# Attention with mixed heads and a folded expert layer on Trainium2: how the first block's score rows reach the softmax

## The chip, the cores and the metric

The kernel runs on one core of a Trainium2 chip. The metric is the device time of one execution in microseconds (us); three executions of the kernel before gave 1636.96, 1638.15 and 1639.79 us, a median of 1638.15 us. A core has TensorE (PE in the rows; PEld is its weight load), VectorE (DVE), ScalarE (ACT), GpSimd (POOL) and SyncE (SP, which in this kernel issues every transfer), and 16 DMA engines that all queues share.

## The reference

```python
scores = scale * np.matmul(q, k.transpose(0, 1, 3, 2))          # batch 8, heads 12, seq 448, dim 64
scores = np.einsum('bhij,hg->bgij', scores, w_pre)              # heads are mixed ahead of the softmax
scores = scores - np.max(scores, axis=-1, keepdims=True)
attn = np.exp(scores)
attn = attn / (np.sum(attn, axis=-1, keepdims=True) + 1e-09)
attn = np.einsum('bhij,hg->bgij', attn, w_post)                 # and mixed again behind it
x = np.matmul(attn, v) -> (3584, 768)
out = (((x @ w1) * (x @ w2)) @ w3) @ w_out                      # 768 -> 1024 -> 1024 -> 768
```

Inputs and result of the attention are float32; the expert weights arrive as 64-bit floats and are converted on the chip.

## The kernel before, in words

**The work is cut into steps.** One step handles 10 query rows of one batch with all 12 heads, so 120 rows of 448 scores; a batch has 45 steps (the code calls `t` a block of 10 rows, and the steps run on over 8 batches to N = 360). To mix heads, the 120 rows must lie on 120 partitions in the order (row, head). The scores are made per head with the query rows on the partitions, so they are written to a buffer in HBM, `raw_d[b]`, of the layout (row, head, column), and read back: `fetch(n)` (L209 to L218) loads the 10 x 12 rows of step n into the rows' tile `r`. In step n the main loop (L890 to L987) issues `fetch(n + 4)`, does `softmax(n)` (a row minimum on VectorE, L246, and an exponential on ScalarE, L249), `scale(n - 1)` (L258 to L262 on VectorE), `post(n - 2)` (four matmuls, L272, and a copy to `mt`, L278) and, last on TensorE, `mix(n + 1)` (L235 in the first 20 steps). All engines work their own instructions strictly in the order of the program.

**Batch 0 starts differently.** Its queries and keys come in six tiles `kq0s`, one for each pair of heads: a first part with the keys and the first 112 query rows (L773), and the other query columns later (`others(p)`, L866 and L867). `qk_first(p, c, banks)` (L149 to L168) makes the scores of pair p and of the c-th 112 query rows: two matmuls (L158), two copies from PSUM (L163 on ScalarE, L164 on VectorE for c = 0), and it hands back the store to `raw_d` (issued at L168). For c = 0 the copies go to one large tile, the score tile `sz` (112 rows x 12 heads x 448). Of it only the first 48 rows (FIRST) are stored by the six stores of L168; the store of the other 64 rows, one transfer of 1344 KB, is the line L800 (`held`). The stores for c = 0 trail the scores by two pairs (L792). The scores with c = 1 to 3 are made inside the main loop: the list `firsts` (L801 to L803) says which in which step. The first one of a step comes ahead of the other matmuls of the step, the others ahead of `mix`.

**Beside it runs the conversion of the weights**, `converting` (L124 to L145), one job in each step: a load of raw words on SP (`cs`, L96, three buffers, two jobs ahead), a square on ScalarE (L102) that waits for that load, four operations on VectorE (L112 to L116) and a step later a cast on ScalarE (L121) and a subtraction on GpSimd (L122). A job has two halves: the load, the cast and the subtraction of the job before, and the square are the first; VectorE's four operations are the second. In a step the first half stands ahead of `softmax(n)` (L944 against L947), the second behind `scale` (L961).

**Order on SP before the main loop**: six first parts of `kq0s`, the two mixing matrices (`wpre`, `wpo`), words of jobs 0 and 1; stores of pairs 0 to 3; words of job 2; stores of pairs 4 and 5; `others(0)`, `others(1)`; `fetch(0)`, `fetch(1)`, `fetch(2)`; words of job 3 (the first marked `wo`); the 1344 KB store; words of job 4; `fetch(3)`; `others(2)`. Step 0 begins with `fetch(4)`, which reads rows 40 to 49 and so waits for both kinds of stores.

Of the kernel before, what the change touches and what calls it, by code (L numbers as in the profile page):

```python
# [6 lines left out]
F32 = mybir.dt.float32  # L7
# [8 lines left out]
B, H, S, D = 8, 12, 448, 64  # L16
DM, FF = 768, 1024
HP = H // 2
IB = 10
GI = H * IB  # L20
NB = -(-S // IB)
JT, NJ = 112, 4
# [23 lines left out]
class Kernel:  # L46
# [102 lines left out]
    def qk_first(self, p, c, banks):  # L149


        nc, t = self.nc, self.kq0s[p]
        cols = slice(c * JT, (c + 1) * JT)
        q = slice(S + cols.start, S + cols.stop) if c else slice(0, JT)
        ps = [self.bank(i, f"psz{p}_{c}_{s}")[:JT, :S] for s, i in enumerate(banks)]
        for s in range(2):
            rows = slice(s * D, (s + 1) * D)
            nc.tensor.matmul(ps[s], t[rows, q], t[rows, JT:JT + S], start=True, stop=True)  # L158
        if c == 0:
            st = self.sz[:, 2 * p:2 * p + 2]  # L160
        else:
            st = (self.qp if p % 2 else self.kp).tile([JT, 2, S], F32, tag="st", name=f"sz{p}_{c}", bufs=2)
        nc.scalar.copy(st[:, 0], ps[0])  # L163
        (nc.scalar.copy if c else nc.vector.tensor_copy)(st[:, 1], ps[1])  # L164
        dst = self.raw_d[0][cols, 2 * p:2 * p + 2, :]
        if c == 0:
            dst, st = dst[:FIRST], st[:FIRST]
        return lambda: nc.sync.dma_start(dst, st)  # L168

# [572 lines left out]
    def run(self):  # L742
        nc, tc = self.nc, self.tc
# [29 lines left out]
            nc.sync.dma_start(self.kq0s[p][:, :JT + S], self.kq0[p][:, :JT + S])  # L773
        self.sz = self.mp.tile([JT, NJ, H, GB * IB], F32, tag="mt", name="sz")
        self.sz = self.sz.rearrange("p j g i -> p (j g i)")[:, :H * S].rearrange("p (h j) -> p h j", h=H)
        w = self.kp.tile([128, S], F32R, tag="qh", name="wpre_s").bitcast(F32)[:GI, :GI]
        self.wsc = cp.tile([GI, GI], F32, name="wsc")
        nc.sync.dma_start(w, self.wpre)
# [8 lines left out]
        self.wph = cp.tile([GI, GI], F32R, name="wph")  # L787
        self.wpl = cp.tile([GI, GI], F32R, name="wpl")
        held = []
        for p in range(HP):  # L790
            held.append(self.qk_first(p, 0, ((0, 1), (2, 3), (6, 7))[p % 3]))
            if p > 1:  # L792
                held.pop(0)()
        nc.vector.tensor_copy(self.wph, self.wsc)
        nc.vector.tensor_tensor(self.wpl, self.wsc, self.wph.bitcast(F32), op=ALU.subtract)
# [4 lines left out]
        held = lambda: nc.sync.dma_start(self.raw_d[0][FIRST:JT], self.sz[FIRST:])  # L800
        firsts = {}  # L801
        for u in range(HP, HP * NJ):
            firsts.setdefault((u - HP) * 15 // (HP * NJ - HP), []).append((u % HP, u // HP))  # L803

# [1 line left out]
        for b in range(1, B):  # L808
            first, per, ahead = (12, 26 / 48, 2) if b == 1 else ((b - 1) * NB - 6, 45 / 48, 3)
            for u in range(H * NJ):  # L810
                h, c = divmod(u, NJ)
                n = first + int(u * per)
# [10 lines left out]
        N = B * NB  # L823
# [29 lines left out]
        def advance(count):  # L853
            nonlocal done
            for _ in range(min(count, total - done)):
                next(background)
                done += 1

        def there(p):

            f, r = divmod(p - 3 - 2 * KF, 3)
            return 2 * KF * 3 * (1 + f) + (0, 9, 18)[r] if f >= 0 else min(max(3 * (p - 3), 0), KF * 3)

        wanted, LF, turn = 0, 4, itertools.chain((6, 7, 0) * 9, itertools.cycle((6, 7)))
        self.v_list = [(b, a, g) for b in range(B) for a in range(NG) for g in range(HP)]
        def others(p):  # L866
            nc.sync.dma_start(self.kq0s[p][:, JT + S:], self.kq0[p][:, JT + S:])  # L867

        others(0)
        others(1)  # L870
        for n in range(LF - 1):
            self.fetch(n)
        next(fold_pieces)
        next(fold_pieces)
# [15 lines left out]
        for n in range(N + 6):  # L890
            self.step = n
            if n == GB + 1:
                self.close("qp")
                self.xp = [self.pool("xp0", 1)]
            if n == SWITCH:
                assert done == total
                next(background, None)
                self.do_ends()
                self.do_soon()
                self.do_later()  # L900
                assert not fold_pieces
                self.close("fp")
                self.wp = self.pool("wp", 5, side="right")
                self.up = self.pool("up", 1, side="right")
                self.xp.append(self.pool("xp1", 1, side="right"))
                background, total, done = self.experts(phases), (E_1 + E_2) * ONE + P_1 * (B - ONE) // 2, 0
            if n == LATE:
                assert done >= E_1
                self.close("xp0", "cx")
                self.xq, self.cb = self.pool("xq", 2), self.pool("cb", 1)  # L910
            if n == PAIR:

                assert done >= 2 * E_1 + E_2 and unit_pieces is None and not self.jobs and not self.ys
                self.do_ends()
                self.do_soon()
                self.do_later()
                self.pairs, self.w_ahead = True, 4
                self.close("xp1", "cb", "xq", "cs")
                self.xq = self.pool("xq", 2)
                self.up2 = self.pool("up2", 1, side="right")  # L920
                self.free += range(N_UP, NS)
                setup = self.pair_setup(phases)
            if PAIR <= n < PAIR + 7:
                next(setup, None)
            if LF <= n + LF < N:
                self.fetch(n + LF)
            self.do_later()
            if n + 3 < HP:
                others(n + 3)
            elif 2 * HP - 3 <= n < 2 * HP:  # L930
                self.load_v()
            for x in loads.get(n, []):
                self.load_kq(*x)
            for x in splits.get(n, []):
                self.split_kq(*x, nc.gpsimd, nc.gpsimd)

            p, pieces = self.n_made - 1 if fold_pieces else 2 * KF + 3 * KF, None
            if avs.get(n):
                pass
            elif fold_pieces:  # L940
                f = (self.n_made - 1 - 2 * KF) // 3
                if f < 2 or done >= 2 * KF * 3 * (f - 1):
                    pieces = fold_pieces
                    if next(pieces, self) is self:  # L944
                        fold_pieces = pieces = None
            if n < N:
                self.softmax(n)  # L947
            if 0 <= n - 1 < N:
                self.scale(n - 1)
            if n + 2 < N:  # L950
                self.split_r(n + 2)
            self.do_soon()
            for x in firsts.get(n, [])[:1]:
                self.later.append(self.qk_first(*x, (next(turn), next(turn))))
            for x in qks.get(n, []):
                store = self.qk(*x, nq % 2, nc.scalar.copy)
                nq += 1
                if store:
                    self.later.append(store)
            if pieces:  # L960
                next(pieces)  # L961
            elif unit_pieces and not fold_pieces and not avs.get(n):
                ahead = 1 if n < SWITCH else 2 * done // (3 * K1) + 4 + (done > 0)
                if n_pieces < ahead:
                    n_pieces += 1
                    if next(unit_pieces, self) is self:
                        unit_pieces = None
                    else:
                        next(unit_pieces)
            now = share.get(n, 0)  # L970
            if n < SWITCH:

                wanted += now
                now = max(min(there(p), KF * 3 + wanted) - done, 0)
            self.do_sums()

            advance(now // 2)
            if 0 <= n - 2 < N:
                self.post(n - 2)
            for x in firsts.get(n, [])[1:]:  # L980
                self.later.append(self.qk_first(*x, (next(turn), next(turn))))
            for x in avs.get(n, []):
                self.av(*x)
            advance(now - now // 2)
            if n + 1 < N:
                self.mix(n + 1)
            self.do_ends()  # L987
# [68 lines left out]
```

## Time and profile before

| | |
|---|---|
| median of three runs | 1638.15 us (1636.96 to 1639.79) |
| the profiled execution | 1639.43 us, span 1637.7 us, so 1.7 us lie around the span |
| mean granted clock of TensorE | 0.993 of full speed |
| TensorE busy | 1579.9 us, 96% of the span |
| GpSimd, VectorE, ScalarE busy | 1068.5, 1030.6, 997.3 us (65%, 63%, 61%) |
| DMA | 446.10 MB, mean 272 GB/s, all on one queue |

A row of a group gives the engine, the line, the operation and the tiles (out<-in), how often it came, and its busy time; in brackets stands the idle time of the engine before it and what ended it. "SPq" is SP's queue: its times are those of issuing a transfer, not of moving the data. PEclk 1.00 is 2.4 GHz, 0.50 is 1.2 GHz.

### The profile page before, as it was taken

The page shows a single profiled execution, that of the slowest core. Times are in us where ns is not written, and L with a number is a line of the kernel's source. Part 1 is how long each engine was busy: PE and PEld are TensorE (multiplying, and loading weights), DVE is VectorE, ACT ScalarE, POOL GpSimd, SP SyncE. Part 2 cuts the span into 40 slices and gives each one's busy share as a digit, 9 for nine tenths or more (in the row PEclk, how much of TensorE's full clock was granted, in tenths as well). Part 3 has the DMA queues.
Part 4 walks back from the last instruction along what each step waited for, and adds up shares of the span by engine and source line. Part 5 has one row for each costly group of instructions (what it writes and reads, how often), then busy time and mean ns, then how long its engine had stood idle before and what let it go on. Part 6 is the DMA issues. An engine that isn't in the chain of part 4 may idle for free. (4 is left out here: it accounts for less than half of the span.)

```text
span 1637.7 us, 31687 instructions
## 1 busy us (share of the span) xinstructions
PE 1579.9 (96%) x10528; PEld 1414.0 (86%) x10528; DVE 1030.6 (63%) x2302; ACT 997.3 (61%) x2413; POOL 1068.5 (65%) x902
## 2 busy tenths in 40 slices
PE   5999999999999999999999999999999999999999
PEld 2578997887898888889899898899999898999988
DVE  5967768778747767863465565745555557634573
ACT  4877657677666776776666666666765554542321
POOL 1346546667657788885576776876675666655774
PEclk7999999999999999999999999999999999999999
DMA  8988879898899999999978977889978756678875
GB/s 263 342 269 275 255 223 302 277 310 288 264 279 310 321 341 315 323 335 306 312 240 279 290 243 238 257 270 309 305 248 250 238 188 196 211 229 302 281 233 179
DMA packets 233906, 446.10 MB, mean 272 GB/s; under 512 B 21838, under 2 KB 159054, under 8 KB 233678
## 3 DMA queue, kind: packets, MB, share of 16 engines
q1 hardware_dynamic: 233742, 444.08, 84.6%
q8 instruction: 83, 1.36, 0.4%
q14 instruction: 81, 0.66, 0.1%
HBM read 309.90 MB, written 134.09 MB: 271 GB/s over the span
## 5 line engine op out<-in xcount | busy, mean ns | idle before, releaser
L227 POOL TENSOR_TENSOR rl<-r,rh 120x448 fp32r<-120x448 f32 (+1 forms) x340 | 425.0, 1250 | 321.9 <-DVE rh L226 108.0
L246 DVE TENSOR_REDUCE mn<-psm 120x1 f32<-120x448 f32 x360 | 223.8, 622 | 410.1 <-PE psm L240 395.1
L249 ACT ACTIVATE e<-psm,mn 120x448 f32<-120x448 f32 x360 | 228.5, 635 | 348.1 <-DVE sa L258 293.4
L272 PEld LDWEIGHTS pso<-w,e 120*112 120x112 f32 (+1 forms) x2880 | 345.5, 177 | 49.4 <-ACT mt L278 35.0
L272 PE MATMUL pso<-w,e 120*112 120x120 f32 (+1 forms) x2880 | 358.9, 267 | 20.6 <-ACT mt L278 20.2
L703 PE MATMUL e<-eh,wu 128*128 128x448 f32 x1008 | 304.4, 371 | 1.1 <-DVE c L657 1.1
L278 ACT COPY mt<-pso 112x480 f32<-112x480 f32 x360 | 206.9, 575 | 14.9 <-PE pso L272 9.9
L703 PEld LDWEIGHTS e<-eh,wu 128*128 128x128 f32 x1008 | 187.3, 188 | 16.1 <-DVE c L657 1.9
L226 DVE CAST rh<-r 120x448 fp32r<-120x448 f32 (+1 forms) x340 | 189.9, 559 | 4.1 <-DMA r<-raw_d 3.0
L703 PE MATMUL e<-el,wu 128*128 128x448 f32 x504 | 187.6, 372 | 2.4 <-POOL el L642 2.4
L198 ACT COPY st<-psq 112x448 f32<-112x448 f32 x336 | 173.3, 527 | 25.8 <-DMA raw_d<-st 25.7
L303 PE MATMUL psa<-mt,v 112*64 112x150 f32 (+1 forms) x2304 | 156.9, 292 | 1.9 <-DMA v<-v 1.9
L183 POOL TENSOR_TENSOR ql<-kq,qh 128x448 fp32r<-128x448 f32 x84 | 99.2, 1181 | 85.1 <-ACT qh L181 84.9
L303 PEld LDWEIGHTS psa<-mt,v 112*64 112x64 f32 x2304 | 143.6, 137 | 8.1 <-DMA v<-v 2.3
L657 DVE TENSOR_TENSOR c<-c,e 128x448 f32<-128x448 f32 x168 | 101.2, 615 | 70.4 <-PE e L703 65.8
L193 PE MATMUL psq<-kk,qh 128*112 128x448 f32 x336 | 125.7, 374 | 8.0 <-ACT st L198 7.8
L238 PE MATMUL psm<-rh,wph 120*120 120x448 f32 (+1 forms) x340 | 129.6, 381 | 0.0
L523 PE MATMUL eg<-xh,wu 128*128 128x448 f32 x384 | 127.3, 381 | 0.0
L240 PE MATMUL psm<-rl,wph 120*120 120x448 f32 (+1 forms) x340 | 124.1, 365 | 0.6 <-POOL rl L227 0.5
L239 PE MATMUL psm<-rh,wpl 120*120 120x448 f32 (+1 forms) x340 | 124.2, 365 | 0.0
L194 PE MATMUL psq<-kk,ql 128*112 128x448 f32 x336 | 122.8, 365 | 0.0
L642 POOL TENSOR_TENSOR el<-x,eh 128x448 fp32r<-128x448 f32 x90 | 105.7, 1195 | 9.3 <-DMA x<-x_d 5.3
(114 smaller groups left out, 2961.7 us busy)
## 6 DMA issues: line engine op xcount, KB each, us to landing
r<-raw_d SPq DMA_DIRECT2D x352, 210.0 KB, 4.1
raw_d<-st SPq DMA_DIRECT2D x168, 392.0 KB, 4.7
wu<-w_d SPq DMA_DIRECT2D x104, 384.0 KB, 5.6
wu<-s_d SPq DMA_DIRECT2D x96, 384.0 KB, 4.4
v<-v SPq DMA_DIRECT2D x144, 224.0 KB, 5.1
kq<-kq SPq DMA_DIRECT2D x42, 672.0 KB, 7.0
wu<-w_d SPq DMA_DIRECT2D x51, 512.0 KB, 5.9
wu<-s_d SPq DMA_DIRECT2D x36, 512.0 KB, 4.4
```

The source lines that it names most:

```text
L193: nc.tensor.matmul(p, qh[:, cols], kk, start=True, stop=False)
L198: copy(st[:, c % 2], p)
L226: nc.vector.tensor_copy(rh[:K], r[:K])
L227: nc.gpsimd.tensor_tensor(rl[:K], r[:K], rh[:K].bitcast(F32), op=ALU.subtract)
L238: nc.tensor.matmul(p[:K, :S], self.wph[:K, :K], rh[:K], start=True, stop=False)
L246: nc.vector.tensor_reduce(mn[:K], p[:K, :S], axis=AX.X, op=ALU.min)
L249: nc.scalar.activation(e[:K], p[:K, :S], AF.Exp, bias=mn[:K], scale=-1.0, accum_out=sm[:K])
L272: nc.tensor.matmul(p[:, j, :, :w], e[:K, j * JT:(j + 1) * JT], w2[:K, :, :w], start=True, stop=True)
L278: self.ends.append((4, lambda: copy(dst, p[:, :, :, :w])))
L303: nc.tensor.matmul(self.psa[rows, g % 3, :W], v[:, j, rows], mt[:, j, 2 * g + s, :W], start=(j == 0), stop=(j == NJ - 1))
L523: nc.tensor.matmul(p, u[:, k % (K1 // 2), x], xs[y][:, k], start=(k == 0 and t == 0), stop=(k == K1 - 1 and t == 2))
L703: nc.tensor.matmul(p, w[:, k, x], ops[m, k][y], start=(k == 0 and t == 0), stop=(k == nk - 1 and t == 2))
```

## The change

Four edits.

- The rows of step 0 no longer go through HBM. After the scores of pair p are copied for c = 0, each of its two heads sends its first 10 rows of the score tile to partitions h, h + 12, ... of the rows' tile `rs[0]`. That makes twelve transfers of 10 x 1792 bytes, the even heads issued by GpSimd, the odd ones by SP. `fetch(0)` is left out. `raw_d` is still written in full.
- The stores of the first 48 rows trail the scores by three pairs, not two; and `others(0)` is issued ahead of `wpre`, not behind the stores.
- In `firsts` the second set of scores with c = 1 (pair 1) moves from step 0 to step 1; all later ones stay in their steps.
- In steps 0 to 3 `softmax(n)` stands ahead of the first half of the conversion job.

```diff
@@ qk_first
         dst = self.raw_d[0][cols, 2 * p:2 * p + 2, :]
         if c == 0:
+
+            for h in range(2 * p, 2 * p + 2):
+                (nc.sync if h % 2 else nc.gpsimd).dma_start(self.rs[0][h::H], self.sz[:IB, h])
             dst, st = dst[:FIRST], st[:FIRST]
         return lambda: nc.sync.dma_start(dst, st)
@@ run
         self.sz = self.sz.rearrange("p j g i -> p (j g i)")[:, :H * S].rearrange("p (h j) -> p h j", h=H)
+        nc.sync.dma_start(self.kq0s[0][:, JT + S:], self.kq0[0][:, JT + S:])
         w = self.kp.tile([128, S], F32R, tag="qh", name="wpre_s").bitcast(F32)[:GI, :GI]
...
         held = []
+        self.rs[0] = self.rp.tile([GI, S], F32, tag="r", name="r0", bufs=3)
         for p in range(HP):
             held.append(self.qk_first(p, 0, ((0, 1), (2, 3), (6, 7))[p % 3]))
-            if p > 1:
+            if p > 2:
                 held.pop(0)()
...
         for u in range(HP, HP * NJ):
-            firsts.setdefault((u - HP) * 15 // (HP * NJ - HP), []).append((u % HP, u // HP))
+            firsts.setdefault((u - HP - 1) * 14 // (HP * NJ - HP - 1) + 1, []).append((u % HP, u // HP))
...
-        others(0)
         others(1)
-        for n in range(LF - 1):
+        for n in range(1, LF - 1):
             self.fetch(n)
...
                 self.split_kq(*x, nc.gpsimd, nc.gpsimd)
+            if n < 4:
+                self.softmax(n)
...
-            if n < N:
+            if 4 <= n < N:
                 self.softmax(n)
```

## Rows read from the trace of the kernel before

**Rows 1.** The page: busy share (PE) and DMA share in 40 equal slices.

```profile
PE   5999999999999999999999999999999999999999
DMA  8988879898899999999978977889978756678875
```

**Rows 2.** Windows: us, busy PE, PEld, DVE, ACT, POOL, PEclk, DMA share, GB/s.

```profile
0.00:10.00 10.00, 6.26 (x17) 2.91 (x19) 1.75 (x4) 2.88 (x4) 0.20 (x4) 1.00 0.81 264
10.00:16.70 6.70, 1.96 (x11) 0.71 (x7) 5.68 (x13) 3.00 (x6) 0.67 (x1) 1.00 0.85 202
18.30:24.10 5.80, 3.92 (x8) 1.42 (x8) 1.92 (x5) 0.83 (x3) 1.72 (x2) 0.55 1.01 290
29.30:33.50 4.20, 1.61 (x4) 0.48 (x4) 2.52 (x5) 1.16 (x3) 0.00 (x0) 0.50 0.75 165
31.80:37.20 5.40, 5.31 (x10) 1.41 (x10) 2.44 (x7) 2.46 (x6) 1.00 (x1) 0.50 0.97 286
33.50:64.00 30.50, 30.32 (x143) 16.74 (x142) 25.64 (x58) 23.33 (x55) 7.02 (x7) 0.94 0.99 341
130.00:1600.00 1470.00, 1440.30 (x9832) 1317.86 (x9833) 927.36 (x2074) 909.33 (x2213) 1011.02 (x845) 1.00 0.86 273
```

**Rows 3.** Timeline of TensorE, 17 to 45 us.

```profile
20.18 1.82 PE L235 MATMUL psm<-r,wsc 120*120 120x448 f32 x2 [8.21 <-DMA r<-raw_d]
21.93 2.54 PE L158 MATMUL psz<-kqz 64*112 64x448 f32 x6
...
26.71 1.64 PE L235 MATMUL psm<-r,wsc 120*120 120x448 f32 x2
31.89 1.84 PE L158 MATMUL psz<-kqz 64*112 64x448 f32 x4 [3.54 <-DMA kqz<-kq]
```

**Rows 4.** Timeline of SP's queue, 0 to 30 us: issues.

```profile
9.08 2.67 SPq L168 DMA_DIRECT2D raw_d<-sz  x4
...
12.84 1.36 SPq L168 DMA_DIRECT2D raw_d<-sz  x2
...
17.39 1.25 SPq L217 DMA_DIRECT2D r<-raw_d  x3
...
19.15 0.61 SPq L800 DMA_DIRECT2D raw_d<-sz  x1
...
20.43 2.21 SPq L217 DMA_DIRECT2D r<-raw_d  x1
22.68 2.52 SPq L867 DMA_DIRECT2D kqz<-kq  x1
```

**Rows 5.** DMA issues near 13, 19 and 22.7 us: KB each, us to landing.

```profile
raw_d<-sz SPq DMA_DIRECT2D x2, 168.0 KB, 3.7
...
raw_d<-sz SPq DMA_DIRECT2D x1, 1344.0 KB, 10.1
...
kqz<-kq SPq DMA_DIRECT2D x1, 168.0 KB, 9.1
```

**Rows 6.** Timeline of VectorE, 8 to 36 us.

```profile
8.24 0.22 DVE L786 TENSOR_SCALAR wsc<-wpre_s 120x120 f32<-120x120 f32 x1 [8.24 <-DMA wpre_s<-wpre]
...
10.50 2.13 DVE L164 COPY sz<-psz 112x448 f32<-112x448 f32 x3 [0.44 <-PE psz L158]
...
19.37 0.42 DVE L116 SCALAR_TENSOR_TENSOR cx<-cm,ca 128x256 f32<-128x256 f32 x1
...
24.16 0.56 DVE L112 TENSOR_SCALAR ca<-cs 128x384 int32<-128x384 int32 x1 [1.50 <-DMA cs<-wo]
```

**Rows 7.** Waits in the first 45 us: total, times, longest.

```profile
ACT cm L102 <- DMA cs<-wo: 8.4, 4, 3.9
```

**Rows 8.** Timeline of ScalarE, 19 to 45 us.

```profile
24.14 0.55 ACT L102 ACTIVATE cm<-cs 128x384 f32<-128x384 f32 x1 [3.91 <-DMA cs<-wo]
...
40.47 0.55 ACT L102 ACTIVATE cm<-cs 128x384 f32<-128x384 f32 x1 [0.83 <-DMA cs<-wo]
40.92 0.62 ACT L249 ACTIVATE e<-psm,mn 120x448 f32<-120x448 f32 x1
```

## The prediction

> **What bounds the kernel now.** I read the page's slices first. TensorE is busy at nine tenths or more in every slice but the first, of 41 us [rows 1]. The stretches say the same closer: from 130 to 1600 us TensorE is busy for 1440.3 of 1470 us, and every step of that part hangs on the one before it on TensorE [rows 2]. So a change at the start is worth what it moves TensorE's long run forward or back, and nothing else; no edit here touches the work of that run. A difference of 0.2%, 3.3 us, is about what a measurement of this kernel can tell from no change.
>
> Next I looked for the point where TensorE's run begins. Its timeline has four pieces early on: the mix of step 0 at 20.18 us, which waited for the rows of `fetch(0)`; scores; the mix of step 1 at 26.71; and, at 31.89, the scores of pair 2 [rows 3]. Ahead of the last it stood idle for 3.54 us until `kqz`, the load that `others(2)` issues, had landed. From there it hardly stops: 5.31 of 5.40 us busy up to 37.2 us, though at 1.2 GHz, and 30.32 of 30.50 us after that, mostly at 2.4 GHz [rows 2]. The landing of `others(2)` is thus **the gate** of the start. What lies ahead of it may come earlier without moving it: step 1's mix ended at 28.35, 3.5 us early.
>
> Then I asked what makes the gate late. SP issued `others(2)` at 22.68, and it landed 9.1 us later, at 31.8 [rows 4, 5]. In between the queue had to move the 1344 KB of the rest of the score tile, issued at 19.15 and landed 10.1 us later, and behind it the words of job 4 and `fetch(3)`. These in turn stand behind `fetch(0)`, which SP could issue only at 17.39: it waits until the last of the six small stores, issued at about 13.8, has landed 3.7 us later [rows 4, 5]. The chain of the start is therefore: last score copy, last small store, its landing, the fetches, the big store, `others(2)`, TensorE. ScalarE and VectorE are not on it.
>
> **The change, part by part.**
>
> *Direct rows.* Twelve transfers come in, six of them on SP, each behind the copy of its own head. An SP issue of a store of the same kind took 0.67 us with its wait (four in 2.67) [rows 4]; six of them and their waits stand in SP's order ahead of stores. The stores suffer from that: the first one, issued at 9.08, now stands behind the row of head 7, which is copied by the first of the three VectorE copies that start at 10.50, so it ends at about 11.2 [rows 6]. `others(0)`, put ahead of `wpre`, makes this later still: its 168 KB take 0.65 us at the 264 GB/s of that stretch [rows 2], and VectorE's first instruction waits for `wpre` [rows 6]; part of that is caught up where VectorE waited 0.44 us for TensorE, so I take 0.4. The first store goes at about 11.9, and then SP works off what is left in its order: the rows of heads 9 and 11, two stores, the words of job 2, three stores. The last VectorE copy ended at 12.63 [rows 6], now 13.0; behind it come the row of head 11 (0.4), a store (0.4), words (0.4) and three stores (1.3), where issues took 0.33 to 0.9 us. The last store is then issued at 15.5 to 15.8 and not at 13.8. **Cost: 1.9 us** on the chain. Its lower bound is 0.9 (all SP issues at 0.33 us, the earlier ones hidden in waits); the upper one 2.6, if all six new issues are paid at 0.67, less the 1.4 that SP spent waiting between the first four stores (2.67 less four issues of 0.33) and can now spend on them.
>
> *GpSimd's half.* No row of before shows GpSimd issue a transfer. From below the price is SP's 0.33 us, from above the time of one of its own subtractions, 0.86 us (two in 1.72 from 18.3 to 24.1 [rows 2]); I take 0.9, since it is the same engine. The last even head is copied at about 12.5, so its row is on its way at 13.4 and lands at about 17, with the 3.7 us of a small store. GpSimd has next to nothing to do up to 16 us [rows 2], so nothing is queued behind it. The mix of step 0 can then start at 17 rather than 20.18. That gain is not on the chain: the gate swallows it. If it came late instead, it would be covered up to about 25.9 us, because the mix of step 0, the scores behind it and the mix of step 1 took 1.82, 2.54 and 1.64 us, 6.0 together, and the gate is at 31.89 [rows 3].
>
> *`fetch(0)` left out.* SP saves 0.42 us (three issues in 1.25), and the queue loses 210 KB. At 290 GB/s, the rate of that stretch [rows 2], this is 0.74 us. By the time that the four transfers from 17.39 to the landing of job 3's words at 24.1 took (6.7 us for three times 210 KB and 128 x 384 words of 8 bytes, 1014 KB [rows 4, 8]) it is 1.4 us. Between them, **gain 1.1 us**. The twelve new transfers carry the same bytes, but while the queue waits for stores anyway.
>
> *Softmax ahead of the conversion, steps 0 to 3.* ScalarE's squares waited four times, 8.4 us in all, for words of weights, and the exponential stood behind each [rows 7]. The first wait ended at 24.14, the fourth at 40.47 [rows 8]. Now the exponentials of steps 0 to 3 go first. Those of steps 0 and 1 come 3 us earlier, and nobody is waiting: their first reader on TensorE is `post(0)`, in step 2, behind the gate. In step 3 the exponential starts where the row minimum ends, some 0.7 us ahead of 40.92; but there the cast and the square, which used to run beside that minimum, come 0.7 to 1.1 us later, and the score copies behind them too. I take 0, with bounds of -0.7 and +0.7. VectorE's order does not change, since the second half of a job already stood behind the minimum; and its work for job 3 still begins when the words land at 24.16 [rows 6].
>
> *`firsts`.* The matmuls of pair 1 go from step 0 into step 1, ahead of the gate both times. One store of 392 KB moves a step later on SP; the queue holds enough beside it. 0, covered by the idle 3.54 us [rows 3].
>
> **Sum:** +1.9 - 1.1 + 0 + 0 = +0.8 us on the gate, and all that follows it moves with it. The profiled execution took 1639.43 us and would take 1640.2; the median of the three runs lies 1.3 us below that execution, so I give **1639.0 us** against 1638.15. Bounds of the terms: 0.9 - 1.4 - 0.7 = -1.2 and 2.6 - 0.74 + 0.7 = +2.6, so 1637 to 1640.8.
>
> The Trainium skill, "DMA: Bandwidth & Descriptors", section "Rules for kernel authors", speaks against the first edit: many small transfers should be made one large one, as below 64 KB one pays mostly overhead, and each new transfer has 17.5 KB where `fetch(0)` had 210. With its fixed cost of about 2 us for each transfer, twelve paid one after the other would be 24 us, an estimate by that page. The trace here only has stores of 168 KB that land 3.7 us after an issue while the next is issued 0.67 us later [rows 4, 5], so landings overlap; that is against paying it twelve times.
>
> **The rivals.**
>
> *A, the queue is the bound (faster).* From 33.5 to 64 us the DMA share is 0.99 at 341 GB/s [rows 2]. If that queue and not TensorE paces the steps there, then what counts is how well it is filled earlier. It moved 202 GB/s from 10.0 to 16.7 us and 165 from 29.3 to 33.5. Filled at 341 these stretches would give back 6.7 x 139/341 = 2.7 and 4.2 x 176/341 = 2.2 us: 4.9 us, 1633.3 us. For it: the 0.99, and one fetch less to wait for. Against: the edits put waits for copies ahead of the stores in just the first of these stretches.
>
> *B, SP's order (slower).* The stores go as late as the upper bound says, 2.6 us, the copies of step 3 lose 0.7, and TensorE, which came to 2.4 GHz 5.3 us after it began to run at 31.89 [rows 2, 3], gets there that much later, with 3.3 us of work at half speed, so 1.6 us more: with 0.7 saved for the fetch, +4.2 us, 1642.4. It decides from the point where the last small store is issued later than about 16.4 us. For it: SP's strict order. Against: issues of 0.33 us are common.
>
> *C, the change does not do what it says (slower).* The twelve transfers write one tile in interleaved rows. If each waits for the landing of the one before, they take 12 x 2.8 us or more (3.7 for a store), and the mix of step 0 starts near 40 us. Less the cover up to 25.9 us this is about +14 us, 1652 us. Nothing in the trace of before shows such a wait or rules it out.
>
> **How the numbers follow.** The forecast, within 3.3 us of before, has 0.54; A 0.19; B 0.21; C 0.06. Everything in A that counts is faster by over 0.2%, so 0.19 and 0.01 from the forecast's own edge: 0.20. B and C are slower by over 0.2%: 0.27, from which I take 0.01 for mild cases of B. So 0.20, 0.54, 0.26. The range takes in the forecast's bounds, most of A and B and leaves C out: 1633.5 to 1643.0 us. The likeliest case's own range is 1635 to 1641.4.
>
> **What would show it.** Right: the last small store of L168 issued near 15.6 us; the mix of step 0 near 17; no wait for words ahead of the first four exponentials; and still an idle stretch of TensorE ended by `kqz` near 32.5. Wrong: the scores of pair 2 start well before 31 us (A), or the idle stretch ahead of them is ended by the mix of step 1 or by the rows' tile (B with late rows, C), or a stall further on that is there now is gone.

## The result, and the profile after

The kernel after takes 1645.82 us, the median of six runs (1641.73 to 1647.39); the kernel before took 1638.40 us in six runs beside it. The ratio is 1.0037, with a 95% interval of 1.0023 to 1.0052: 6.1 us (3.8 to 8.5) slower. That is beyond the predicted range. The profiled execution took 1647.39 us, with a span of 1645.6 us.

I read the same views in the same order. First the windows of the kernel after (columns as in [rows 2]; the second one is the whole start):

```profile
10.00:16.70 6.70, 2.10 (x10) 0.84 (x6) 6.12 (x13) 2.47 (x5) 2.09 (x4) 0.91 0.43 96
...
0.00:24.10 24.10, 11.83 (x30) 4.38 (x30) 10.73 (x22) 7.85 (x15) 6.24 (x13) 0.82 0.69 201
33.50:64.00 30.50, 28.40 (x129) 15.20 (x129) 25.11 (x57) 22.61 (x54) 7.05 (x7) 0.90 0.98 327
130.00:1600.00 1470.00, 1438.69 (x9803) 1316.04 (x9802) 924.16 (x2074) 904.66 (x2204) 1002.76 (x840) 1.00 0.86 273
```

The long run reads as before. The start does not: from 10.0 to 16.7 us the queue moves 96 GB/s where it moved 202 [rows 2], and over the first 24.1 us 201 where the same window of the kernel before has 247. That is 46 x 24.1 = 1.1 MB less, 3.3 us of the queue at 341 GB/s. By itself this does not show that the queue's bytes set the pace; two experiments below bear on that.

TensorE's timeline of the kernel after answers to [rows 3]:

```profile
17.60 1.82 PE L238 MATMUL psm<-r,wsc 120*120 120x448 f32 x2 [5.50 <-DMA raw_d<-sz]
...
24.52 1.85 PE L238 MATMUL psm<-r,wsc 120*120 120x448 f32 x2 [3.33 <-DMA r<-raw_d]
...
35.39 1.84 PE L158 MATMUL psz<-kqz 64*112 64x448 f32 x4 [4.98 <-DMA kqz<-kq]
```

Step 0's mix starts at 17.60 instead of 20.18 (of what arrives by transfer here it reads only the rows' tile; the store in its row is what by the profile came last), step 1's at 24.52 instead of 26.71, and all of that is lost again: TensorE then stands idle for 4.98 us and begins pair 2 at 35.39, 3.5 us later than before. Why, stands in SP's queue (start, time of the issues, count), against [rows 4]:

```profile
9.56 3.38 SPq L169 DMA_DIRECT2D r<-sz  x4
13.04 0.41 SPq L171 DMA_DIRECT2D raw_d<-sz  x1
13.55 0.73 SPq L169 DMA_DIRECT2D r<-sz  x1
...
14.89 0.74 SPq L169 DMA_DIRECT2D r<-sz  x1
...
16.71 1.53 SPq L171 DMA_DIRECT2D raw_d<-sz  x3
...
21.83 0.77 SPq L220 DMA_DIRECT2D r<-raw_d  x2
...
23.11 0.59 SPq L805 DMA_DIRECT2D raw_d<-sz  x1
...
25.80 2.41 SPq L872 DMA_DIRECT2D kqz<-kq  x1
```

The six transfers from score tile to rows' tile take 3.38 + 0.73 + 0.74 us to issue, some 0.8 us each, and the stores stand behind them. It is SP and not the copies that sets this pace: VectorE has copied head 7 by about 11.5 us, and SP is done with that head's row at 12.94. The first store goes at 13.04 (9.08 before) and the last at 16.71 + 2 x 0.51 = 17.7 (13.8). The fetches wait for its landing and go at 21.83 (17.39), the 1344 KB store at 23.11 (19.15), `others(2)` at 25.80 (22.68). Transfers issued from 16.6 to 18.2 us and from 25.8 to 26.6 us show the landings, 4.0 and 9.5 us against 3.7 and 9.1 in [rows 5]:

```profile
raw_d<-sz SPq DMA_DIRECT2D x3, 168.0 KB, 4.0
...
kqz<-kq SPq DMA_DIRECT2D x1, 168.0 KB, 9.5
```

VectorE's timeline has its first instruction and the score copies behind it, against [rows 6]:

```profile
8.78 0.22 DVE L790 TENSOR_SCALAR wsc<-wpre_s 120x120 f32<-120x120 f32 x1 [8.78 <-DMA wpre_s<-wpre]
8.92 3.84 DVE L164 COPY sz<-psz 112x448 f32<-112x448 f32 x6
```

The waits of the first 45 us have ScalarE's square waiting twice for words, 7.0 us in all, against [rows 7]:

```profile
ACT cm L102 <- DMA cs<-wo: 7.0, 2, 4.6
```

ScalarE's timeline has the third exponential ahead of the square that it used to follow, against [rows 8]:

```profile
39.70 0.63 ACT L252 ACTIVATE e<-psm,mn 120x448 f32<-120x448 f32 x1 [1.50 <-DVE mn L249]
...
40.72 0.56 ACT L102 ACTIVATE cm<-cs 128x384 f32<-128x384 f32 x1
```

The copies end at 12.76 (12.63 before), so neither engine is what makes the stores late; and the exponential waits for its row minimum, no longer for words.

To see what of the start reaches the steps, I take a **landmark**: the first subtraction on GpSimd that splits the rows for the mix (used behind the first 20 steps). The view by tile gives it for before and after (ns of the shortest, median and longest; when the first begins):

```profile
L227 POOL TENSOR_TENSOR rl<-r,rh x4: 1143/1146/1157, 107.6 to 120.2; 120x448 fp32r<-120x448 f32 x4
```

```profile
L230 POOL TENSOR_TENSOR rl<-r,rh x4: 1141/1144/1153, 110.9 to 123.4; 120x448 fp32r<-120x448 f32 x4
```

It is 3.3 us late; what TensorE lost at the start (3.5 us at pair 2) arrives there. One profile places it only to about 2 us. In a second profile of the kernel before it begins at 107.7, and in the run with probes behind the kernel's end (below), whose computation is that of the kernel before, at 109.7:

```profile
L227 POOL TENSOR_TENSOR rl<-r,rh x4: 1138/1144/1149, 109.7 to 122.3; 120x448 fp32r<-120x448 f32 x4
```

### The profile page after: what moved, and what is told of

The parts are those of the page before. It is cut to its first block, busy times and chain, and to the rows that moved or that the text cites. A ratio compares the mean times of both kernels' runs of the same rounds, so it can differ in the third digit from the quotient of the medians.

```text
span 1645.6 us, 31721 instructions
## 1 busy us (share of the span) xinstructions
PE 1586.8 (96%) x10528; PEld 1418.6 (86%) x10528; DVE 1027.8 (62%) x2302; ACT 997.4 (61%) x2413; POOL 1071.3 (65%) x908
```

## The experiments

All results first. "Landmark" is its shift against the kernel before's 107.6 us, each from one profile, so that shifts below some 2 us may be scatter; us are the ratio less 1, times 1638.

| run | landmark, us | ratio (95%) | us |
|---|---|---|---|
| the change | +3.3 | 1.0037 (1.0023 to 1.0052) | +6.1 |
| the change again | +4.0 | 1.0035 (1.0022 to 1.0047) | +5.7 |
| without the direct rows | +1.1 | 0.9999 (0.9986 to 1.0012) | -0.2 |
| all twelve by GpSimd | +3.4 | 1.0030 (1.0019 to 1.0042) | +4.9 |
| all twelve by SP | +7.6 | 1.0054 (1.0042 to 1.0067) | +8.8 |
| SP's six behind the stores | +3.6 | 1.0016 (1.0004 to 1.0028) | +2.6 |
| twelve late on GpSimd | +7.9 | 1.0054 (1.0040 to 1.0068) | +8.8 |
| the change, old place of softmax | +5.3 | 1.0038 (1.0025 to 1.0052) | +6.2 |
| before, only softmax moved | -0.1 | 1.0004 (0.9993 to 1.0014) | +0.7 |
| before again | +0.1 | 0.9998 (0.9984 to 1.0011) | -0.3 |
| before, `others(2)` early | +0.6 | 1.0003 (0.9992 to 1.0015) | +0.5 |
| before, `others(2)` to `(4)` early | +0.9 | 1.0012 (1.0000 to 1.0024) | +2.0 |
| before, `fetch(4)` late | +0.5 | 0.9994 (0.9984 to 1.0004) | -1.0 |
| before, stores late | +0.9 | 0.9998 (0.9987 to 1.0009) | -0.3 |
| both waits eased | -0.4 | 0.9991 (0.9982 to 1.0001) | -1.5 |
| three edits | -1.6 | 0.9996 (0.9985 to 1.0007) | -0.7 |
| three edits again | -1.9 | 0.9993 (0.9980 to 1.0005) | -1.1 |
| four edits | -2.4 | 0.9991 (0.9978 to 1.0003) | -1.5 |

### Which part of the change costs the time

**The change without the direct rows** (the other three edits stay):

```diff
-            for h in range(2 * p, 2 * p + 2):
-                (nc.sync if h % 2 else nc.gpsimd).dma_start(self.rs[0][h::H], self.sz[:IB, h])
...
-        for n in range(1, LF - 1):
+        for n in range(LF - 1):
```

> The changed kernel without the twelve direct transfers: step 0's rows come by fetch(0) again. The stores still trail by three pairs, others(0) is still early, firsts and the softmax order are as changed. Theory G: the last small store is issued at 13.8 to 14.5 us, pair 2 starts at 31.8 to 32.8 us, and the kernel takes 1638 to 1640.5 us. Rival S, or a loss that comes from firsts or the trailing stores: 1643 to 1647 us.

Measured: no difference, 0.9999. The stores' later trail, `others(0)` ahead of `wpre` and the new `firsts`, with the new place of softmax, together cost nothing that shows (the landmark, 1.1 us late, is within its scatter). The loss is that of the direct rows.

**The change with softmax in its old place, and before with only softmax moved** (the lines taken out of the one are put into the other):

```diff
-            if n < 4:
-                self.softmax(n)
...
-            if 4 <= n < N:
+            if n < N:
```

> The changed kernel with the softmax of steps 0 to 3 back behind the first half of the conversion job. Theory G: pair 2 still starts at 35 to 36 us and the time stays within 1 us of the changed kernel, 1645 to 1647 us. Rival S: back to 1638 to 1641 us.

> The kernel before with one edit of the four: in steps 0 to 3 the softmax stands ahead of the first half of the conversion job. Theory G (only the landing of others(2), which starts pair 2, counts): pair 2 still starts at 31.5 to 32.5 us and the time stays within 1.5 us of before. Rival S: the four waits for words, 8.4 us in all, are on the path, and the kernel gets 2 to 5 us faster; or the late cast and square cost 1 to 3 us.

Measured: 1.0038 against 1.0037 of the change, and 1.0004 on the kernel before. In neither does the time differ measurably. The landmark is 2.0 us later in the first, without the move, and 0.1 us earlier in the second, with it: by one profile each, the move may be worth something once the start is late. 2.0 us is no more than the landmark's scatter, so that is not shown.

**All twelve by GpSimd, and all twelve by SP:**

```diff
-                (nc.sync if h % 2 else nc.gpsimd).dma_start(self.rs[0][h::H], self.sz[:IB, h])
+                nc.gpsimd.dma_start(self.rs[0][h::H], self.sz[:IB, h])
```

> All twelve direct transfers are issued by GpSimd, none by SP; the rest as in the changed kernel. Theory G (the loss is SP's issues of 0.72 to 0.90 us for each ten-row transfer, which make the last small store late): the last small store is issued at 13.5 to 14.5 us and not at 17.8, the scores of pair 2 start at 31 to 32.5 us and not at 35.4, and the kernel takes 1637 to 1641 us. Rival S (the loss is the exponential ahead of the conversion on ScalarE): the start of pair 2 may move, the time stays at 1644 to 1647 us. Rival P (GpSimd's own queue, 0.52 us an issue, makes the rows late): the mix of step 0 starts after 20 us.

> All twelve direct transfers are issued by SP, none by GpSimd; the rest as in the changed kernel. Theory G: six more issues of 0.74 us, some of them inside SP's waits for copies, so the last small store goes 2 to 4.4 us later than 17.8 us, pair 2 starts at 37 to 40 us, and the kernel takes 1647 to 1651 us. Rival S: no change from the changed kernel, 1645 to 1646 us. Rival P (GpSimd's part is what costs): faster than the changed kernel, 1638 to 1642 us.

By SP the cost grows as the issues do: eight of them (8.56 us with their waits for copies) stand ahead of the first store, which goes at 15.52. The last goes at 22.1, 4.4 us later than in the change, and the landmark is 4.3 us later too; 1647.4 us is at the lower edge of what was expected.

```profile
6.91 8.56 SPq L169 DMA_DIRECT2D r<-sz  x8
15.52 0.46 SPq L171 DMA_DIRECT2D raw_d<-sz  x1
```

By GpSimd, SP has none of them to issue, and yet most of the loss stays. SP's queue, and the transfers issued from 12.9 to 18.2 us:

```profile
9.98 1.36 SPq L171 DMA_DIRECT2D raw_d<-sz  x3
...
13.02 4.92 SPq L171 DMA_DIRECT2D raw_d<-sz  x3
```

```profile
raw_d<-sz SPq DMA_DIRECT2D x3, 168.0 KB, 5.8
...
r<-sz POOLq DMA_DIRECT2D x6, 17.5 KB, 5.3
```

Three stores now take 4.92 us to issue and land 5.8 us later (3.7 before), so the fetches go at 21.68, as late as in the change. The step 0 mix starts at 21.75, past the 20 us that the third theory named, but it is not what holds the start: pair 2 begins at 35.03, and the 5.18 us ahead of it are ended by `kqz` as before. The first theory's 31 to 32.5 us and 1637 to 1641 us both failed. Moving the issues does not move the cost away: the small transfers and the stores hold each other up. The same three stores, behind the same words, without any direct rows and beside GpSimd's six (the first experiment, and the one with SP's rows behind the stores):

```profile
12.50 1.72 SPq L169 DMA_DIRECT2D raw_d<-sz  x3
```

```profile
12.49 2.69 SPq L169 DMA_DIRECT2D raw_d<-sz  x3
```

So 1.72, 2.69 and 4.92 us to issue beside none, six and twelve, and 3.5, 4.2 and 5.8 us to land. GpSimd's transfers land 5.3 us after their issue here and 2.1 us in the change, the medians of six, where fewer were under way. The Trainium skill says why splitting over engines could not be enough: "DMA: Bandwidth & Descriptors", section "Issuing engines are not separate DMA queues", has it that transfers of all engines interleave on the same 16 DMA engines, and that issuing from several of them saves only issue time. The trace agrees as far as sharing goes: the stores' landing grows from 3.5 to 5.8 us. Their issue on SP grows as well, from 0.57 to 1.64 us each.

### Is it the issue or the transfer?

**All twelve behind the last small store in the program,** still half on each engine, ahead of `others(1)`. On GpSimd this moves nothing, since nothing stands between: its six go from 6.43 to 12.24 us, where they were 6.32 to 12.28. Only SP's six come later:

```diff
-            for h in range(2 * p, 2 * p + 2):
-                (nc.sync if h % 2 else nc.gpsimd).dma_start(self.rs[0][h::H], self.sz[:IB, h])
...
+        for h in range(H):
+            (nc.sync if h % 2 else nc.gpsimd).dma_start(self.rs[0][h::H], self.sz[:IB, h])
```

> The changed kernel with its twelve direct transfers (six on SP, six on GpSimd as before) issued behind the last small store and not in between. Theory Q (the loss is that the DMA queue runs empty from 10 to 17 us, because the stores wait on SP behind the ten-row transfers and their copies; every later step is late by as much as the queue is late in bytes): the queue moves 190 to 220 GB/s from 10 to 16.7 us in place of 96, the last small store is issued at 13.8 to 14.5 us, steps 4 to 20 are within 1.2 us of before, and the kernel takes 1637 to 1640 us, although the mix of step 0 starts at 20 to 22 us and not at 17.6. Rival D (ten-row transfers cost the queue wherever they stand): steps 4 to 20 are 2 to 4 us late, 1641 to 1645 us.

The stores are out in time now, the last issued at 14.3, but SP pays for its six issues all the same, and what stands behind them is late (SP's queue):

```profile
15.24 5.49 SPq L804 DMA_DIRECT2D r<-sz  x6
...
21.30 0.88 SPq L218 DMA_DIRECT2D r<-raw_d  x2
```

5.49 us for six, 0.92 each. The fetches go at 21.30, the landmark is 3.6 us late, and the time is 2.6 us above before: less than in the change, but not even. From 10.0 to 16.7 us the queue moves 201 GB/s again, as in the kernel before, so theory Q fails in the form in which it was put: the thin queue of that stretch is not what costs. Rival D's figures came, 2 to 4 us late and 1641 to 1645 us. SP is what the fetches wait for here: the stores had landed by about 18.5 us, and SP was issuing rows until 20.7.

**The price by itself:** behind the last store of the kernel, four issues of each kind in a row, in one run; the rest of the computation is unchanged.

```diff
+        for i in range(4):
+            nc.sync.dma_start(ya[i:i + 109:H, i], x[:IB])
+        for i in range(4):
+            nc.sync.dma_start(yb[:IB, i], x[:IB])
...
```

> The kernel before, with probes behind its end: groups of four transfers of 1792 bytes a row, on SP 10 rows to every 12th partition, 10 rows to 10 partitions, 16 rows to 16, then 10, 16 and 48 rows to HBM, and on GpSimd 10 and 16 rows. Theory R (the 0.72 us of an issue on SP comes with the number of rows, 10, which is no multiple of 16): both forms of 10 rows within SBUF and the 10 rows to HBM take 0.65 to 0.9 us an issue, those of 16 and 48 rows 0.3 to 0.45. Rival (it comes with SBUF as the target, or with every 12th partition): 10 rows to HBM take 0.3 to 0.45, or only the first group takes 0.7. GpSimd: 0.5 to 0.55 us for both.

SP's queue, in this order: to every 12th partition, 10 rows and 16 rows side by side within SBUF, 10, 16 and 48 rows to HBM, and one load of 48 rows from HBM back into SBUF; then GpSimd's, 10 and 16 rows within SBUF:

```profile
1638.50 3.19 SPq L1010 DMA_DIRECT2D pa<-px  x4
1641.74 2.96 SPq L1012 DMA_DIRECT2D pb<-px  x4
1644.74 2.47 SPq L1014 DMA_DIRECT2D pc<-px  x4
1647.25 1.62 SPq L1016 DMA_DIRECT2D pd<-px  x4
1648.92 1.69 SPq L1018 DMA_DIRECT2D pe<-px  x4
1650.66 1.81 SPq L1020 DMA_DIRECT2D pw<-px  x4
1654.20 0.30 SPq L1022 DMA_DIRECT2D pv<-pw  x1
```

```profile
1656.87 2.25 POOL L1024 DMA_DIRECT2D pf<-pv  x4 [28.51 <-DMA pv<-pw]
1659.10 1.95 POOL L1026 DMA_DIRECT2D pg<-pv  x4
```

On SP 0.80, 0.74 and 0.62 us each within SBUF, 0.40 to 0.45 to HBM whatever the number of rows; on GpSimd 0.56 and 0.49. From the same tile, a destination in SBUF makes SP's issue dear and one in HBM does not. A destination in SBUF alone does not do it: the load from HBM took 0.30 us, and the fetches of the kernel before 0.42 each [rows 4]. As far as these kinds show, it is both ends in SBUF. So theory R (the ten rows) failed; the ten rows and the stride of twelve add a little.

**Late on GpSimd:** all twelve in the program behind `fetch(2)` and the next job of the conversion, so on GpSimd behind its first subtraction:

```diff
-            for h in range(2 * p, 2 * p + 2):
-                (nc.sync if h % 2 else nc.gpsimd).dma_start(self.rs[0][h::H], self.sz[:IB, h])
...
+        for h in range(H):
+            nc.gpsimd.dma_start(self.rs[0][h::H], self.sz[:IB, h])
```

> The changed kernel with all twelve direct transfers on GpSimd, behind its first subtraction, so that they start at about 17 us, behind the issue of the small stores, and SP issues none. Theory I (SP's issues of transfers within SBUF, 0.7 to 0.9 us each, are the loss, and beside the stores such transfers slow the stores down): the last small store is issued at 13.5 to 14.5 us, the 1344 KB store at 18.5 to 20 us in place of 23.1, steps 4 to 20 within 1.2 us of before, 1637 to 1640 us, though the mix of step 0 starts at 24 to 26 us. Rival D (these transfers cost the queue 3 us wherever they stand and whoever issues them): the 1344 KB store at 21.5 us or later, steps 2.5 to 4 us late, 1641 to 1644 us.

```profile
33.82 1.82 PE L236 MATMUL psm<-r,wsc 120*120 120x448 f32 x2 [20.75 <-DMA r<-sz]
```

SP is free here: the last three stores take 1.76 us to issue, and its 1344 KB store goes at 20.27. But GpSimd's transfers, issued from 18.08 on, run beside that store and land 9.0 us after their issue, and step 0's mix waits until 33.82. That is 7.9 us past the 25.9 up to which the prediction had it covered, and the landmark is 7.9 us late. The cover was worked out right, from its other side. The times of both theories were missed: neither had the rows' own landing on the path.

### Is the landing of `others(2)` the only gate?

**`others(2)` issued behind the fetches, ahead of the 1344 KB store, in the kernel before:**

```diff
+        others(2)
         held()
...
-        others(2)
```

> The kernel before with others(2) issued ahead of the 1344 KB store and not behind it; nothing else. Theory G: the load lands at 25 to 27 us, the idle 3.5 us of TensorE ahead of pair 2 go, pair 2 starts at 28.3 to 29.5 us; the next thing that is late is others(3), behind the wait for the 1344 KB store, so pair 3 starts 1.5 to 2.7 us earlier than 35.4 us, and the kernel takes 1635 to 1637 us. Rival A (the DMA queue's filling paces the steps up to 64 us): pair 2 starts earlier, but step 10 is not earlier than before by more than 0.5 us, and the time stays.

Pair 2 and the next mixes on TensorE:

```profile
29.19 1.84 PE L158 MATMUL psz<-kqz 64*112 64x448 f32 x4
...
38.54 1.01 PE L158 MATMUL psz<-kqz 64*112 64x448 f32 x4 [2.41 <-ACT fo L121]
...
40.94 0.92 PE L235 MATMUL psm<-r,wsc 120*120 120x448 f32 x2
```

The gate opens 2.7 us earlier (29.19 for 31.89), the idle stretch is gone, and at 38.54 TensorE stands idle for 2.41 us instead; the landmark is 0.6 us late and the time 1.0003. Another wait lay right behind: TensorE waits for a cast of ScalarE, and the square ahead of that cast had waited 1.95 us for words. Issuing `others(2)` to `others(4)` early, ahead of the same store, was no better:

```diff
+        others(2)
+        others(3)
+        others(4)
         held()
...
-        others(2)
...
-            if n + 3 < HP:
-                others(n + 3)
+            if n + 5 < HP:
+                others(n + 5)
```

> The kernel before with others(2), others(3) and others(4) issued ahead of the 1344 KB store. Theory G: pair 2 starts at 28.3 to 30 us and pair 3 at 32 to 33 us in place of 35.4; the 1344 KB store lands 1 to 2 us later, and with it fetch(4); the kernel takes 1634.5 to 1637 us. Rival A: the same bytes in the queue, so no gain at step 10, 1637.5 to 1639.5 us.

1.0012, with its landmark 0.9 us late.

**What stood behind** is `fetch(4)`: SP waits at it until the 1344 KB store has landed, from 25.2 to 29.31 us in the kernel before, with the later `others` and words in its order behind. So it was issued behind step 0's work instead of ahead of it:

```diff
-            if LF <= n + LF < N:
+            if LF < n + LF < N:
...
+            if n == 0:
+                self.fetch(LF)
```

> The kernel before, with fetch(4), which makes SP wait for the 1344 KB store, issued in step 0 behind others(3) and the words of job 5 and not ahead of them. Theory Q: SP hands the queue 550 KB some 4 us earlier, so the 165 GB/s between 29.3 and 33.5 us rise to 220 or more, and steps 4 to 20 come 0.8 to 2.2 us earlier: 1635 to 1637 us. Rival G (only others(2) counts): steps 4 to 20 stay within 0.5 us.

Alone this gives nothing either (0.9994, landmark +0.5), although the queue now moves 290 GB/s from 29.3 to 33.5 us where it moved 165. More bytes early did not bring the steps early. **Both at once,** and both with softmax ahead of the squares in steps 0 to 3:

> The kernel before with both edits that moved nothing alone: others(2) ahead of the 1344 KB store, and fetch(4) of step 0 behind the words of job 5. Theory T (two chains leave the same queue, one by others(2) to TensorE, one by SP's wait at fetch(4) to the words and others(4), and each alone holds the steps): together they let steps 4 to 20 come 1 to 2.5 us earlier, and the kernel takes 1635 to 1637.5 us. Rival Q alone (the queue's bytes set the pace whatever their order): steps 4 to 20 within 0.6 us of before, no change of the time.

> The two edits of the run with both waits early, and the softmax of steps 0 to 3 ahead of the conversion. Theory T: exponentials no longer wait for words once TensorE is early, so steps 4 to 20 come 1.5 to 3 us earlier, 1634.5 to 1637 us: faster than both kernels. Rival Q alone: within 0.6 us of before.

TensorE in the kernel with both waits eased and nothing else:

```profile
37.77 1.01 PE L158 MATMUL psz<-kqz 64*112 64x448 f32 x4 [1.86 <-DMA kqz<-kq]
...
41.07 1.67 PE L235 MATMUL psm<-r,wsc 120*120 120x448 f32 x2
```

TensorE in the kernel with three edits:

```profile
34.90 0.92 PE L235 MATMUL psm<-r,wsc 120*120 120x448 f32 x2
...
39.43 0.92 PE L235 MATMUL psm<-r,wsc 120*120 120x448 f32 x2
```

With both waits eased the landmark is only 0.4 us early, short of the 1 to 2.5 that were expected. The scores at 37.77 were at 39.52 in the kernel before, but from 39 to 43 us TensorE's granted clock is 0.57, where it is 1.00 in the kernel before and with three edits, and the mix at 41.07 is no earlier than with `others(2)` early alone (40.94). Only with the third edit do the steps come clearly early: the mix at 39.43 was at 41.91 in the kernel before (41.23 and 42.11 in two more profiles of the same computation), and the landmark is 1.6 us early. That freeing one wait shows nothing is measured; that these two alone bound the start is not shown, because easing just these two was not enough in the one profile taken.

**The stores late, in the kernel before:**

```diff
-            if p > 1:
+            if p > 4:
```

> The kernel before with the small stores trailing the scores by five pairs, not two: all else as before, no direct transfer. Theory Q: SP starts the stores at 12 to 12.7 us, the queue moves 100 to 150 GB/s from 10 to 16.7 us, the last small store is issued at 15.3 to 16.3 us and steps 4 to 20 are 1.0 to 2.5 us late: 1639 to 1641 us. Rival D (only the direct transfers cost): steps 4 to 20 within 0.7 us of before.

This one did not make them late: with no direct rows on SP nothing else stands between the stores, and the last went out at about 13.4. What moved was the load of job 2's words, ahead of most of them. So the question that it was built for, what late stores alone cost, was not answered by it. The same line was then tried as a fourth edit, beside the three again:

> The kernel with three edits (the other parts of pair 2 behind the first fetch, fetch(4) behind step 0's work, exponentials ahead of the squares in steps 0 to 3), and the six small stores begin behind pair 5's scores, so that the words of job 2 stand ahead of most of them. If two waits of SP bound the start together: steps 4 to 20 come 2 to 3.5 us early and the time is 1634.5 to 1636.5 us. If the start doesn't reach the end: within 1 us of the kernel before, with the steps early all the same.

> The kernel with three edits once more. If its early steps reach the end: again 1.0 to 2.5 us below the kernel before. If they don't: within 1 us of it.

The landmarks are 2.4 and 1.9 us early; the times, 0.9991 and 0.9993, stay within what can be told from no change. In the three profiles with the third edit the landmark is earlier than in any of the three of the kernel before's computation, so the early steps repeat. All four runs with both waits eased lie 0.7 to 1.5 us below before, and each interval takes in 1. **No version was shown to beat the kernel before.**

### Does the result repeat, and how far do executions scatter?

> The changed kernel, unchanged, for a second profile and more runs. Theory I: the start repeats (1344 KB store at 22.7 to 23.5 us, steps 4 to 20 2.8 to 3.7 us late), and the time is 1641 to 1646 us; what the first profile lost behind step 60 (4.5 us) is the scatter between executions and is not all there again: its second profile loses between -3 and +4 us there. Rival L (a loss of the change's own behind the start): again 3 us or more behind step 60, and a ratio of 1.0035 or more.

> The kernel before, unchanged, for a second profile: how far the start of pair 2 (31.9 us) and the later steps move from one execution to the next. Expected: pair 2 within 0.7 us of 31.9, step 60 within 1.5 us, the end within 3 us.

The change repeats: 1.0035, landmark +4.0. The kernel before in a second profile has the same landmark (+0.1) but a span of 1642.9 us for 1637.7: 5 us that come behind the start, without any edit, and more than the 3 us that were expected. Part of them can be seen at TensorE's clock. At about 404 us TensorE waits 1.7 us for a copy of ScalarE in both executions of this one kernel. The timeline of TensorE and a window (columns as in [rows 2]) of the first execution:

```profile
403.79 1.02 PE L272 MATMUL pso<-w,e 96*112 96x96 f32 x8 [1.70 <-ACT mt L278]
418.94 1.07 PE L272 MATMUL pso<-w,e 120*112 120x120 f32 x8 [1.13 <-ACT mt L278]
```

```profile
404.00:408.00 4.00, 4.00 (x36) 3.66 (x37) 3.17 (x11) 3.38 (x9) 2.37 (x3) 1.00 0.85 278
```

And of the second:

```profile
404.51 1.16 PE L272 MATMUL pso<-w,e 96*112 96x96 f32 x8 [1.71 <-ACT mt L278]
421.22 1.07 PE L272 MATMUL pso<-w,e 120*112 120x120 f32 x8 [1.13 <-ACT mt L278]
```

```profile
404.00:408.00 4.00, 3.49 (x15) 3.17 (x16) 1.94 (x8) 3.01 (x7) 2.33 (x3) 0.66 0.94 302
```

Behind the same idle time the clock stays at 2.4 GHz in the first and falls to 1.2 GHz for a while in the second, and from one of the two waits to the next it takes 15.15 and 16.71 us: 1.6 us for one such stage.

## Why the prediction was wrong

**The failed step** is the first term of the sum, "+1.9 us" for the direct rows: the last small store was to go at 15.5 to 15.8, and went at 17.7. The prediction priced an issue of such a row like a store's, 0.33 to 0.67 us; on this path it measured 0.73 to 0.85, and 0.80 alone. Four of them also stand ahead of the first store, forecast at 11.9 and issued at 13.04. The term is +3.9, beyond the upper bound of 2.6, because that bound too was a store's price: with the measured 0.81 (4.85 us for six) in place of 0.67 it would have been 3.5. The rows have both ends in SBUF, and the trace of before had no issue of that kind; a range for an unseen kind of transfer should not have ended at the dearest issue of the seen kind. With the landing 0.3 us longer it is +4.2.

**"While the queue waits for stores anyway"** failed as well: the run with all twelve by GpSimd shows stores landing 5.8 us after their issue with no direct row on SP. The new bytes were covered, the new transfers were not.

**`fetch(0)` left out,** -1.1: right. The start is 4.2 us late at the landing of the last small store and 3.1 (25.80 for 22.68) at the issue of `others(2)`, so 1.1 came back (0.8 by the second profile). Its landing then took 9.5 us for 9.1, which makes the 3.5 of pair 2.

**GpSimd's half:** priced at 0.9 us, measured 0.53; the mix of step 0 forecast at about 17, measured 17.60, and its gain swallowed at the gate, as said. That the 17 came out is luck: it stood for GpSimd's last row, which was issued at 12.28 and took 1.7 us to land, so it was there by about 14. The row issued last was SP's of head 11, at 14.89, which the prediction had at about 13. The cover to 25.9 us held in the late run.

**Softmax and `firsts`,** 0: right in the time, by the two runs on softmax and by the one without the direct rows; at the landmark the move gave 2.0 us in the changed kernel, past the bound of 0.7, but not clear of the landmark's scatter. `firsts` was not run by itself.

**The gate** was right for this change: TensorE's idle stretch ended by `kqz` is there, at 35.39. It was incomplete for anything that goes the other way: other waits lay just behind it.

**The rivals.** B named the right place: the last small store went later than its 16.4 us. Its size came from other terms, though. SP's order cost 3.9 and not 2.6, softmax 0 and not 0.7, and TensorE's lower clock added nothing by the landmark (+3.5 at pair 2, +3.3 there). A fell: the stretch from 29.3 us filled at 290 GB/s gave nothing back alone. C fell: the twelve landings overlap, and step 0's mix starts at 17.60. A mild form of it shows with all twelve on GpSimd, where the eleventh and twelfth issue waited 0.89 and 0.80 us for the landing of an earlier row.

**What stays open.** The start explains 3.3 to 4.0 us; the runs measure 6.1 (3.8 to 8.5) and 5.7 (3.6 to 7.7). From the landmark to the end of the span the change lost 4.6 us against before in its first profile and 1.2 in its second; the second profile of the kernel before lost 5.1 there. Both profiles of the change have stages at 1.2 GHz behind 250 us, three in each, at about 268, 408 and 1395 to 1398 us; but the kernel before had none in one profile and four in the other. At 1.6 us each they could be the rest. Over the 19 profiles without the probes the stretch behind the landmark is longer the more such stages it has: 1525 to 1531 us with none or one, 1528 to 1532 with two, 1531 and 1535 with three, 1535 with four. That is in keeping with 1.6 us each. Whether a late start makes them more frequent was not shown.

## What to carry to other kernels

Price each new transfer by its kind and by the queue that issues it: here a row from SBUF to SBUF held SP for 0.8 us, twice a store to HBM, and six of them ahead of the stores cost more than the HBM round trip that they saved. Handing the issues to another engine frees the issuer, not the DMA engines. And before a gate is taken as the only bound of a stage, ask what the engine would wait for next: here easing either of two waits alone gave nothing, and the steps came clearly early only with three edits at once.

## What the runs showed that was not expected

- SP's issue within SBUF takes 0.62 to 0.80 us (16 and 10 rows); from SBUF to HBM it takes 0.40 to 0.45 us, for 10 to 48 rows alike, and from HBM to SBUF 0.30 (48 rows).
- Beside twelve transfers of 17.5 KB from GpSimd, SP's issue of three stores grew from 1.72 to 4.92 us, and their landing from 3.5 to 5.8 us; beside six it was 2.69 and 4.2.
- One transfer of 17.5 KB from GpSimd landed after 2.1, 5.3 or 9.0 us (medians of three runs): with six in the change, with twelve beside the small stores, and with twelve beside the 1344 KB store.
- After the same idle time of 1.7 us TensorE's clock fell to 1.2 GHz in one execution of a kernel and not in another, at 1.6 us for a stage.
